# Twelve transfers of a recurrence-and-FFN kernel, issued from ScalarE's queue instead of SyncE's

## The chip, the cores and the metric

The kernel runs on one core of one Trainium2 chip. The metric is the device time of one execution in microseconds; the median of three runs before the change is 415.52 us (415.25 to 416.81). The engines are called PE (TensorE), DVE (VectorE), ACT (ScalarE), POOL (GpSimd) and SP (SyncE). Each engine works through its own list of instructions in order. SP does nothing but issue transfers (DMAs); ACT can issue transfers too, between its other instructions. Each of the two has a hardware queue of its own.

## The reference

The first half is a gated linear recurrence for 4 batches, 8 heads, 768 time steps and a head size of 48; the second half is a feed-forward network on the 3072 resulting rows of 384 features, with the maximum of three products in its middle:

```python
f = 1.0 / (1.0 + np.exp(-f_logit))
for t in range(S):
    state = f[:, :, t, :, None] * state + np.einsum('bhd,bhe->bhde', k[:, :, t], v[:, :, t])
    y[:, :, t] = np.einsum('bhd,bhde->bhe', q[:, :, t], state)
x = y.transpose(0, 2, 1, 3).reshape(B * S, H * D)
h = np.maximum(np.maximum(x @ w1, x @ w2), x @ w3)     # 384 -> 768
return h @ w_out                                       # 768 -> 384
```

The four weight matrices come as 64-bit floats; the kernel rounds them to 32 bits itself.

## The kernel before, in words

**Units and groups.** The recurrence is cut into 24 units. Unit `u` covers a chunk of 64 time steps (`c = u // 2`) of two batches (`bp = u % 2`) for all heads, so 128 tokens. Four units form a group of 512 tokens, which goes through the network together; there are six groups. While units 4 to 7 are worked on, group 0 goes through the network, and so on, one group behind.

**One unit.** `load` (L183) and `load_v` (L164) fetch f, k, q and v. From unit 6 on, f, k and q are fetched for two units at once, as eight transfers each. `sigmoids` (ACT, L311), `scan`, `after` and `before` turn them into the scaled keys `kh` and queries `qh`; DVE scans and transposes, POOL makes the products (L340 for `kh`, L351 for `qh`) and copies chunk ends (L339). `pairs` (PE, L392) multiplies `kh` by `qh`, and DVE masks the result. `values` (PE, L411) multiplies that by v, so it needs the unit's v in place. `sums` (L436) makes the next state. `finish` (PE, L500) adds what the state gives, and three ACT copies (L506) put the result into the group's tile `xT`.

**Packing.** A head has 48 features, but lies on 64 partitions. `xT` has four planes of head pairs; `pack` (L519) moves the 48 rows of the fourth plane into the gaps of the first three, by two transfers inside SBUF, so that the network's products run over three full planes of 128. It is called for units 0 to 2 of a group together and for the fourth alone, each time right after `finish`. `sums_of_x` (POOL, L854) and the network's products (PE, L870) read the packed tile.

**The network for group 0** (`ffn_first`). It runs plain products (L537) while weights are still being rounded. At its end, `place` (L454 and L461) moves the weight differences by transfers inside SBUF into a layout that fits the packed tile: ten transfers into `placed0`, ten into `placed1`, ten into a part of `w_in0`. `outputs` (PE, L563) makes the four output tiles of 128 tokens, numbered 0 to 3; ACT copies each out of PSUM (L567) and `store` (L555) sends it to the output in two transfers. Between the steps of `outputs`, POOL does `mix_in(0)` to `mix_in(3)` (L839, sums and differences of the placed weights; the first reads the first seven transfers into `placed1`), then `mix` (L587) and, during the last tile, `sums_of_x` of group 1.

**The network for groups 1 to 5.** `inputs_by_pairs` and `outputs_by_pairs` (PE, L870 and L631) save multiplications by adding and subtracting blocks beforehand, much of it on POOL. Their output stores go through `store_late`, from SP; the last group has its own, mostly from SP too.

**What sets the order.** The order is written out by hand: the loop over units calls the steps above, and between them `fill(part)` takes as many steps of the network off a list as fit a given PE time. Every engine gets its instructions in this order. Around the change, in the loop for unit 7: `finish(6)`, `pack` of units 4 to 6, `pairs(7)`, loads of f for unit 10 and of v for unit 9, `scan`, `after` and `before` of unit 8, `values(7)`; for unit 8: `finish(7)`, `pack` of unit 7, `pairs(8)`, v of unit 10, `values(8)`, k and q of unit 10. `outputs` of group 0 lie among these on PE, the `place` transfers among them on SP.

**How transfers are counted.** A transfer reports that it has landed by adding 16 to one of eight counters (named DMAHW0 to DMAHW7 in the built program). The tile framework gives the counters out in turn to all transfers of both queues, in one order that it plans when the program is built. A transfer is issued only after the previous transfer on its counter has landed: its queue waits for that count first, and for the data it needs.

## Time and profile before

| | |
|---|---|
| median of three runs | 415.52 us (415.25 to 416.81) |
| the profiled execution | 416.47 us, of which the span of its instructions is 414.6 us |
| granted PE clock, mean | 0.998 |
| busy in the span: PE, PE weight loads, DVE | 397.8, 332.4, 290.8 us |
| busy in the span: ACT, POOL | 178.7, 245.2 us |
| transfers from SP's queue | 178032 packets, 45.62 MB |
| transfers from ACT's queue | 3472 packets, 0.81 MB |

Times in the profile count from the span's first instruction. A line of a timeline gives start, length, engine, line of the program, operation, what it writes and reads, how many instructions are merged, and in brackets the idle time before it with what ended it. "SPq" and "ACTq" are transfers issued by that engine; their length is that of the issue, and the transfer lands later. A line of waits reads: who waited, for whom, microseconds in total, times, the longest.

Issues take their time on the engine that makes them: SP's mostly 0.6 to 0.65 us. From issue to landing, the profile's medians are 2.2 us for an output store, 3.2 for v, 2.6 for the large and 1.9 for the small pack, and 3.4 to 3.7 for the transfers into `placed0` and `placed1`.

### The profile page before, as it was taken

To read this page: it belongs to the slowest core of one execution; us is meant where nothing else is said; L and a number is where in the kernel's file an instruction comes from. 1 tells how busy PE (TensorE), PEld (TensorE's weight loads), DVE (VectorE), ACT (ScalarE), POOL (GpSimd) and SP (SyncE) were. 2 spreads that over 40 slices of the span, in tenths; PEclk is the share of its full clock that TensorE was granted. 3 is DMA by queue.
4 is the path that set the end of the run, shared out by engine and by line. 5 is a ranking of instruction groups with operands and counts; after the bars stand their busy time and mean duration, and the time that the engine had idled before them with its cause. 6 is when DMAs were issued, how large, how long until landed. Compare 5 with 4: busy or idle time off the path is not lost.

```text
span 414.6 us, 11546 instructions
## 1 busy us (share of the span) xinstructions
PE 397.8 (96%) x4598; PEld 332.4 (80%) x4598; DVE 290.8 (70%) x569; ACT 178.7 (43%) x412; POOL 245.2 (59%) x270
## 2 busy tenths in 40 slices
PE   4988999999999999999999999999999999999995
PEld 4766775566668889998889988889988899988984
DVE  6987897996695899898888976988894550002500
ACT  2478786511223531444541354533345324576210
POOL 2189694730989887487496376667466860435700
PEclk9999999999999999999999999999999999999999
DMA  8989987677356767377625376724473011541002
GB/s 170 237 261 273 250 231 93 86 143 159 83 104 96 122 114 132 70 118 89 137 78 104 52 117 86 163 64 80 71 146 96 2 55 44 148 136 60 0 21 62
DMA packets 181562, 47.21 MB, mean 114 GB/s; under 512 B 160448, under 2 KB 179200, under 8 KB 181504
## 3 DMA queue, kind: packets, MB, share of 16 engines
q1 hardware_dynamic: 178032, 45.62, 54.0%
q10 hardware_dynamic: 3472, 0.81, 0.9%
q8 instruction: 37, 0.61, 0.6%
q14 instruction: 21, 0.17, 0.1%
HBM read 37.75 MB, written 4.72 MB: 102 GB/s over the span
## 4 chain that ended last, share of the span: by engine, by line
PE 76%; DVE 6%; SPq 5%; POOL 3%; DMA 3%; ACT 3%; issue 2%; ACTq 0%; POOLq 0%; DVEq 0%
PE p L870 16%; PE p L631 14%; PE tr L870 13%; PE tr L631 11%; PE p L537 6%; PE p L563 3%; PE y L411 3%; PE y L500 2%; PE p L776 2%; SPq L174 2%; DMA raw<-in_moe_w_dram 2%; PE a L392 2%; PE y L436 2%; DVE ks L382 2%; SPq L164 1%
## 5 line engine op out<-in xcount | busy, mean ns | idle before, releaser
L382 DVE STREAM_TRANSPOSE ks<-kh 32x128 f32<-32x128 f32 x256 | 77.4, 302 | 11.9 <-POOL kh L340 7.7
L870 PE MATMUL tr<-xT,placed 128*128 128x256 f32 x300 | 72.6, 385 | 0.3 <-DVE hm L913 0.3
L870 PEld LDWEIGHTS tr<-xT,placed 128*128 128x128 f32 x300 | 55.7, 190 | 9.3 <-ACT hm L878 1.2
L870 PE MATMUL p<-xT,placed 128*128 128x256 f32 x180 | 45.1, 382 | 0.3 <-POOL xT L854 0.3
L339 POOL COPY ends<-r 128x8 f32<-128x8 f32 x24 | 9.8, 407 | 48.5 <-DVE r L329 48.5
L870 PEld LDWEIGHTS p<-xT,placed 128*128 128x128 f32 x180 | 33.7, 190 | 5.3 <-POOL xT L854 0.7
L537 PE MATMUL p<-xT,w_in 128*128 128x256 f32 (+1 forms) x108 | 33.9, 458 | 3.0 <-POOL w_in L745 2.2
L329 DVE TENSOR_TENSOR_SCAN r<-gate,from_one 128x520 f32<-128x520 f32 x24 | 31.5, 1314 | 6.1 <-ACT gate L308 3.0
L340 POOL TENSOR_TENSOR kh<-kt,r 128x512 f32<-128x512 f32 x18 | 30.1, 1671 | 7.6 <-DVE kt L296 6.2
L639 DVE TENSOR_TENSOR o<-tr,w_in 128x384 f32<-128x384 f32 (+1 forms) x11 | 5.7, 521 | 38.6 <-PE tr L631 35.1
L347 DVE TENSOR_TENSOR_SCAN prod<-gate,from_inv 128x520 f32<-128x520 f32 x24 | 32.1, 1336 | 0.0
L603 POOL TENSOR_TENSOR w_in<-hm 128x256 f32<-128x256 f32 x15 | 11.1, 739 | 34.9 <-DVE hm L921 32.2
L506 ACT COPY xT<-y 64x256 f32<-64x256 f32 (+1 forms) x60 | 22.1, 369 | 19.2 <-PE y L500 18.1
L870 PE MATMUL p<-w_in,placed 128*128 128x256 f32 x120 | 30.0, 379 | 0.0
L913 DVE TENSOR_TENSOR hm<-tr,hm 128x512 f32<-128x512 f32 x15 | 10.3, 688 | 26.6 <-PE tr L870 19.7
L537 PEld LDWEIGHTS p<-xT,w_in 128*128 128x128 f32 x108 | 19.5, 190 | 11.8 <-issue 6.0
L636 ACT COPY w_in<-p 128x384 f32<-128x384 f32 x15 | 7.2, 478 | 46.0 <-PE p L631 46.0
L631 PE MATMUL p<-w_in,hm 128*128 128x192 f32 x120 | 25.4, 335 | 1.1 <-ACT w_in L636 1.1
L258 POOL TENSOR_TENSOR w_in<-top_bits,rest_bits 128x384 uint32<-128x384 uint32 x18 | 21.8, 1218 | 7.6 <-DVE top_bits L252 4.7
L280 ACT ACTIVATE raw<-top_bits 128x384 f32<-128x384 f32 x48 | 25.2, 526 | 0.4
L870 PEld LDWEIGHTS p<-w_in,placed 128*128 128x128 f32 x120 | 22.8, 190 | 3.1
L631 PE MATMUL tr<-w_out,w_in 128*128 128x192 f32 x120 | 24.4, 326 | 0.0
(159 smaller groups left out, 907.6 us busy)
## 6 DMA issues: line engine op xcount, KB each, us to landing
raw<-in_moe_w_dram SPq DMA_DIRECT2D x24, 384.0 KB, 3.8
v_ld<-in_v_dram SPq DMA_DIRECT2D x48, 96.0 KB, 3.2
placed<-in_moe_w_dram SPq DMA_DIRECT2D x12, 384.0 KB, 5.4
out_dram<-o SPq DMA_DIRECT2D x46, 96.0 KB, 2.2
placed<-in_moe_w_out_dram SPq DMA_DIRECT2D x6, 384.0 KB, 6.3
f_ld<-in_f_logit_dram SPq DMA_DIRECT2D x36, 64.0 KB, 3.4
k_ld<-in_k_dram SPq DMA_DIRECT2D x36, 64.0 KB, 2.5
q_ld<-in_q_dram SPq DMA_DIRECT2D x36, 64.0 KB, 2.5
```

The costliest lines, as they stand in the source:

```text
L258: nc.gpsimd.tensor_tensor(dst, by(top), by(rest), op=ALU.add)
L280: nc.scalar.activation(over, size, AF.Relu, scale=(-1 / HI_MIN, 1.0)[step - 1], bias=(1.0, -HI_END * (1 - 2.0 ** -24))[step - 1], accum_ou ...
L329: nc.vector.tensor_tensor_scan(r[:, 0:LEN][:, ::-1], flat(gate)[:, ::-1], flat(from_one)[:, ::-1], 1.0, op0=ALU.mult, op1=ALU.max)
L340: (nc.vector if u < BY_ROWS else nc.gpsimd).tensor_tensor(kh.rearrange("p h a t -> p a h t"), kt, by_batch(r[:, 1:LEN + 1].rearrange("p (x ...
L347: nc.vector.tensor_tensor_scan(flat(prod), flat(gate_tiles[u % 2]), flat(from_inv[u % 2]), 1.0, op0=ALU.mult, op1=ALU.max)
L382: nc.vector.transpose(ks[n * 32:(n + 1) * 32, :, par, e0:e0 + 32], kh[p0:p0 + 32, :, a, t0:t0 + 32])
L411: nc.tensor.matmul(y[o:o + DP, a, hp * C:(hp + 1) * C], lhsT=v_ld[s, 2 * hp + par, :], rhs=d["at"][s, par, hp, :], start=(hp == 0), stop=F ...
L506: nc.scalar.copy(xT[o, :, t0 + a * C:t0 + (a + 1) * C], y[i, a, 0:HP * C].rearrange("p (h t) -> p h t", h=HP))
L537: nc.tensor.matmul(p if w < TOK else p.rearrange("p (two t) -> p two t", two=2), lhsT=w_in[i][:, kt, j * 128:(j + 1) * 128], rhs=x[:, t.st ...
L563: nc.tensor.matmul(p[:, 0:DM], lhsT=lhsT, rhs=rhs, start=(n == 0), stop=(n == NJ + NK - 1))
L631: nc.tensor.matmul(b[:, p * HD:(p + 1) * HD], lhsT=x, rhs=w, start=id(b) not in begun, stop=True, skip_group_check=True)
L870: nc.tensor.matmul(b[:, j * HALF:(j + 1) * HALF], lhsT=w[:, (2 * n + j) * 128:(2 * n + j + 1) * 128], rhs=x, start=begin and j == 0, stop= ...
```

## The change

Twelve transfers move from SP's queue to ACT's: the four packing transfers of group 1 (units 4 to 6 together, and unit 7), and the eight output stores of group 0. Each stands in ACT's order right behind the copies that write what it reads. The packs of groups 2 to 5, all other stores and all loads keep their queues, and no other instruction changes its place on its engine.

```diff
-            def store(u, o):
+            def store(u, o, queue=nc.sync):
                 c, bp = divmod(u, 2)
                 for a in range(2):
                     t0 = (2 * bp + a) * S + c * C
-                    nc.sync.dma_start(out=out[t0:t0 + C, :], in_=o[a * C:(a + 1) * C, :])
+                    queue.dma_start(out=out[t0:t0 + C, :], in_=o[a * C:(a + 1) * C, :])
...
                             o = o_four[:, i]
                             nc.scalar.copy(o, p[:, 0:DM])
-                            store(i, o)
+                            store(i, o, nc.scalar)
...
                     if u > GRP:
                         finish(u - 1, xT)
+                        queues = act if u <= 2 * GRP else one
                         if u % GRP == 3:
-                            pack(0, 2, xT)
+                            pack(0, 2, xT, queues)
                         elif u % GRP == 0:
-                            pack(3, 3, xT)
+                            pack(3, 3, xT, queues)
```

`act` is the pair of queues `(nc.scalar, nc.scalar)`, `one` is `(nc.sync, nc.sync)`.

## The prediction

> **What bounds the kernel now.** First the page's engine table and the waits of PE, to see what there is to win; then the timelines of SP, ACT, POOL and PE between 80 and 125 us, where the moved transfers lie.

> Page, part 1, and the longest table of PE's waits after 60 us:
> ```profile
> PE 397.8 (96%) x4598; PEld 332.4 (80%) x4598; DVE 290.8 (70%) x569; ACT 178.7 (43%) x412; POOL 245.2 (59%) x270
> PE tr L870 <- DVE hm L913: 0.3, 1, 0.3
> PE p L870 <- POOL xT L854: 0.3, 1, 0.3
> ```
> PE is full; from 60 to 200 us it waits 0.6 us in all. That is everything a smoother queue can return here, since what follows is PE-bound too.

> SP's queue (start, length, transfers):
> ```profile
> 80.34 5.13 SPq L183 DMA_DIRECT2D q_ld<-in_q_dram  x8
> 85.51 1.28 SPq L164 DMA_DIRECT2D v_ld<-in_v_dram  x2
> 86.97 1.32 SPq L454 DMA_DIRECT2D placed<-w_in  x2
> 88.33 5.04 SPq L461 DMA_DIRECT2D placed<-w_in  x8
> 93.47 1.94 SPq L164 DMA_DIRECT2D v_ld<-in_v_dram  x2
> 95.52 1.27 SPq L454 DMA_DIRECT2D placed<-w_in  x2
> 96.84 5.04 SPq L461 DMA_DIRECT2D placed<-w_in  x8
> 109.44 1.26 SPq L519 DMA_DIRECT2D xT<-xT  x2
> 117.38 2.50 SPq L555 DMA_DIRECT2D out_dram<-o  x4
> 119.97 1.35 SPq L519 DMA_DIRECT2D xT<-xT  x2
> ```
> SP issues without a break at about 0.63 us each, 10 to 18 us behind the ACT copies that it carries away:
> ```profile
> 94.59 1.14 ACT L506 COPY xT<-y 128x256 f32<-128x256 f32 x3 [1.55 <-PE y L500]
> 99.09 0.48 ACT L567 COPY o<-p 128x384 f32<-128x384 f32 x1 [3.36 <-PE p L563]
> 106.17 0.48 ACT L567 COPY o<-p 128x384 f32<-128x384 f32 x1 [6.60 <-PE p L563]
> 108.73 1.14 ACT L506 COPY xT<-y 128x256 f32<-128x256 f32 x3 [1.55 <-PE y L500]
> 349.27 0.70 ACTq L519 DMA_DIRECT2D xT<-xT  x1
> ```
> The last line is the price of an issue on ACT. POOL and PE:
> ```profile
> 104.15 1.81 POOL L839 TENSOR_TENSOR placed<-placed 128x768 f32<-128x768 f32 x1 [13.09 <-DMA w_in<-w_in]
> 107.21 1.18 POOL L351 TENSOR_TENSOR qh<-qt,prod 128x512 f32<-128x512 f32 x1
> 100.92 0.69 PE L411 MATMUL y<-at,v_ld 64*64 64x64 f32 x32
> 108.00 0.67 PE L500 MATMUL y<-qh,state 48*48 48x64 f32 x32
> 108.49 0.65 PE L392 MATMUL a<-qh,kh 48*64 48x64 f32 x32
> ```
> POOL stands 13 us at `mix_in(0)` (L839) for placed weights. Behind it in POOL's order is `qh` of unit 8 (L351), ending at 108.39; PE's `pairs(8)` (L392) takes it at 108.49. So PE has 0.1 us of slack against those placed weights.

> **The change, part by part.** *SP loses 12 issues*, about 7.6 us at 0.63. If nothing else happened the packs would land earlier (POOL's 1.9 us wait at L854 goes), q for unit 10 would come earlier (DVE waits 1.5 us for it), and PE would win back its 0.6 us.

> *ACT gains 12 issues at 0.70*, in pairs of 1.4 us. After the pack at 95.7, the stores of tiles 0 and 1 and the pack at 109.9, ACT idles 3.36, 6.60, 1.55 and 3.36 us: hidden (the 1.55 just). After tile 3 (120.8) it idles 0.85; L311, L884 and L506 slip by up to 0.6. L884 then ends at 123.2 against PE's need of its bank at 124.43: hidden. Without those idles all of it would be 8.4 us. Zero taken.

> *The counters.* This decides. In the built program of the changed kernel every transfer of both queues counts on one of eight counters, given out in turn in the planner's order, and its issue waits until the transfer eight places earlier has landed. Before, all of these were SP's own and long landed. Now ACT's twelve sit in the same row, and well ahead of where ACT really gets to them. A landed transfer adds 16, so the count that a wait asks for, divided by 16, names the transfer. Read so, SP waits for ACT:

> | SP's issue | waits for ACT's |
> |---|---|
> | 7th of 8 of q, units 8 and 9 | pack of units 4-6, first half |
> | v of unit 7, first | same pack, second half |
> | 3rd, 4th of placed0 | stores of tile 0 |
> | 9th of placed0 | store of tile 1, first |
> | v of unit 8, first | store of tile 1, second |
> | 2nd, 3rd of placed1 | pack of unit 7, both halves |
> | 5th of f, unit 10 | store of tile 2, first |
> | 1st, 3rd of k, unit 10 | stores of tile 3 |

> So SP stops after the sixth q, 80.34 + 6 x 0.64 = 84.2, for a pack that ACT can issue only when `finish(6)` is copied. Walked forward:

> 1. Copies end 95.73; packs issued at 95.76 and 96.50. Such a pack took 2.5 us from issue to landing (its second issue at 110): 98.3 and 99.0. SP stood 14 us.
> 2. SP: two q from 98.3, v of unit 7 at 99.65 and 100.3. v took 2.9 at 85: landed 103.2. PE wants it at 100.92: **stall 2.4** (with 2.6, the shortest v, and 1.9, the shortest pack: 1.5; with 3.2, the median: 2.7).
> 3. SP: placed0 from 100.95; stores of tile 0 landed (99.60 and 100.33 plus 2.2), no stop; the 8th goes at 106.5, the 9th waits for tile 1: copied at 106.17 + 2.4 + 0.48 = 109.05, stored at 109.08, landed (2.2) 111.3. Then 10th, v of unit 8 twice, placed1 first: 112.0 to 114.6.
> 4. `finish(7)`: L506 at 108.73 + 2.4, ends 112.27; packs at 112.3 and 113.03, landed (2.0 for the small one) 114.3 and 115.1. SP's 2nd and 3rd of placed1 go at 114.65 and 115.3, the 7th, the last that `mix_in(0)` reads, at 115.3 + 4 x 0.63 = 117.85.
> 5. Before, that 7th went at 99.36 (96.84 + 4 x 0.63) and POOL began 4.8 later; placed transfers landed in 2.9 to 4.4, 3.6 median. I take 3.6 + 0.4 = 4.0, the queue being less full: **L839 at 121.9 instead of 104.15, 17.7 late** (16.0 with the short landings and a stall of 1.5, 18.9 with 4.8 and 2.7).
> 6. POOL's chain to `qh(8)` follows unchanged, 4.24 us: 126.1. PE has reached `pairs(8)` at 110.9 and stands until 126.2. PE is in order, so everything after is 17.7 late; the 2.4 is inside it, since PE had that wait on the way.
> 7. Later waits: with the restart below, all on PE is 19.9 late; the stores of tiles 2 and 3 (copied at about 133 and 140.7) hold SP's f, k and q of unit 10 again; k starts at 140.7 + 2.2 = 142.9, against 124.16 + 19.9 = 144.1 for before's place in the shifted program. No new stall; the lead of POOL remains, so the 0.6 us is won.

> *The cold restart.* PE has never stood 15 us in mid-run. The nearest row is its start after 5 us of idling:
> ```profile
> 5.05 1.08 PE L291 MATMUL tr<-ident,f_ld 128*128 128x128 f32 x4 [5.05 <-DMA f_ld<-in_f_logit_dram]
> 17.92 0.60 PE L291 MATMUL tr<-ident,f_ld 128*128 128x128 f32 x4
> ```
> Groups of four took 1.06 to 1.09 until 9.9 us, 0.60 later: 4.9 us at 0.56 of the rate, 2.2 us lost. The page's clock row shows 9 throughout, so zero is the lower end; I take 2.2, the row of the same engine after idling. [...]

> Sum: 17.7 + 2.2 - 0.6 = **+19.3 us**. The profiled execution took 416.47 (span 414.6 and 1.87 around it), so one like it would take 435.8; the median of runs, 415.52, lies 0.95 lower: **434.8**.

> **The rivals.**
> - *No cold restart* (0.13): the same walk, 415.5 + 17.1 = 432.6. For it, the clock row; against, the slow transposes at the start.
> - *A second hold-up* (0.15): in step 7 the loads of unit 10 have about 1 us in hand. If stores land in 4.2 instead of 2.2, as the pair issued at 122.8 did, each such hop adds 2 us, at tile 1's store (step 3) and again at tile 3's: up to 439.
> - *Only the late v* (0.04): were `mix_in(0)` not held, 415.5 + 2.4 = 418. Against it: POOL's order puts it ahead of `qh(8)`, and it had 0.1 us of slack.
> - *Not slower* (0.06): SP is relieved and its counters do not hold it; 0.6 won, 414.9. Price and point: it needs the 7th of placed1 issued by about 99.4, so the pack of unit 7 landed by 96.9, before `finish(7)` exists (108.7). It holds only if the waits I read belong to other transfers. This is also the case that the change does what it says.

> **How the numbers follow.** The walk above has 0.62. Its own range, all short to all long: 16.0 + 0 - 0.6 to 18.9 + 2.4, so 431 to 437. With the second hold-up and a little for a longer ACT issue: 430 to 439, leaving out the last two rivals and the ends. About 0.5% (2.1 us) is what a measurement of this kernel can tell from no change: faster 0.01, same 0.05, slower 0.94.

> **What would show it.** SP without an issue from about 84 to 98 and from 107 to 111; PE waiting about 2 us at L411 for v and about 15 at L392 for POOL's qh; POOL's wait at L839 near 31 us; L631 or L870 matmuls as long as before; POOL's wait for xT at L854 gone; slow matmuls after the restart. Wrong if SP runs through 84 to 98, or if PE passes L392 without standing: then the counters were misread.

## The result and the profile after

The changed kernel takes 435.18 us (median of four runs, 434.49 to 435.93) against 415.88 us for the kernel before beside it: a ratio of 1.0462, 95% interval 1.0432 to 1.0493. It is 19.3 us slower. The prediction was 434.8 us. The profiled execution took 434.61 us with a span of 432.9 us, 18.3 us more than the span of before.

The page of the changed kernel, busy times and the granted clock of PE in forty slices of the span:

```profile
PE 400.1 (92%) x4598; PEld 333.6 (77%) x4598; DVE 290.0 (67%) x569; ACT 178.7 (41%) x412; POOL 245.0 (57%) x270
...
PEclk9999999999859999999999999999999999999999
```

The work is the same, instruction for instruction in number; PE is busy 2.3 us longer and idle for the rest of the loss. The clock row, flat before, has two low slices (8 and 5), between 108 and 130 us. PE's waits from 60 to 240 us say where the idling is:

```profile
PE a L392 <- POOL qh L351: 14.1, 1, 14.1
PE y L411 <- DMA v_ld<-in_v_dram: 2.2, 2, 1.4
PE tr L870 <- DVE hm L913: 0.3, 1, 0.3
```

One wait of 14.1 us at `pairs(8)` and one of 2.2 us for v stand where before had 0.6 us in all. The cause lies two engines away. SP's queue in the changed kernel (start, length, transfers):

```profile
80.12 18.63 SPq L183 DMA_DIRECT2D q_ld<-in_q_dram  x8
98.79 1.28 SPq L164 DMA_DIRECT2D v_ld<-in_v_dram  x2
100.25 1.32 SPq L454 DMA_DIRECT2D placed<-w_in  x2
102.25 10.04 SPq L461 DMA_DIRECT2D placed<-w_in  x8
112.39 1.40 SPq L164 DMA_DIRECT2D v_ld<-in_v_dram  x2
113.89 1.27 SPq L454 DMA_DIRECT2D placed<-w_in  x2
115.24 5.03 SPq L461 DMA_DIRECT2D placed<-w_in  x8
...
126.70 10.71 SPq L183 DMA_DIRECT2D f_ld<-in_f_logit_dram  x8
```

Eight loads of q took 5.13 us before and 18.63 now, eight transfers into `placed0` 5.04 and 10.04. A merged line's length holds the time in which SP stood between two of its issues. ACT's side of it:

```profile
94.32 1.14 ACT L506 COPY xT<-y 128x256 f32<-128x256 f32 x3 [1.55 <-PE y L500]
95.11 1.39 ACTq L519 DMA_DIRECT2D xT<-xT  x2
...
108.53 0.48 ACT L567 COPY o<-p 128x384 f32<-128x384 f32 x1 [9.22 <-PE p L563]
109.04 1.12 ACTq L555 DMA_DIRECT2D out_dram<-o  x2
```

ACT issues each transfer as soon as the copies that it reads are done. SP's seventh q goes once the first pack of 95.11 has landed (97.90 and 97.89 us in the trace, on the same counter), and its ninth `placed0` once tile 1's store of 109.04 has (111.14 and 111.12). SP's longest waits from 78 to 145 us are for ACT's transfers; before the change none of its waits there was for a transfer:

```profile
SPq L183 <- DMA xT<-xT: 13.7, 1, 13.7
SPq L183 <- DMA out_dram<-o: 8.3, 2, 6.6
SPq L461 <- DMA out_dram<-o: 5.4, 2, 4.8
```

POOL and PE take the delay on:

```profile
120.84 1.80 POOL L839 TENSOR_TENSOR placed<-placed 128x768 f32<-128x768 f32 x1 [30.05 <-DMA placed<-w_in]
```
```profile
125.09 1.13 PE L392 MATMUL a<-qh,kh 48*64 48x64 f32 x32 [14.07 <-POOL qh L351]
126.16 3.70 PE L563 MATMUL p<-w_out,hm 128*128 128x384 f32 x6
```

`mix_in(0)` on POOL starts at 120.84 instead of 104.15, `pairs(8)` on PE at 125.09 instead of 108.49, and the six products after it take 3.70 us instead of 2.20. Before the change they were:

```profile
109.06 2.20 PE L563 MATMUL p<-w_out,hm 128*128 128x384 f32 x6
```

### The profile page after: what moved, and what is told of

Its sections match the earlier page's. It is cut to its first block, busy times and chain, and to the rows that moved or that the text cites. A ratio compares the mean times of both kernels' runs of the same rounds, so it can differ in the third digit from the quotient of the medians.

```text
span 432.9 us, 11549 instructions
## 1 busy us (share of the span) xinstructions
PE 400.1 (92%) x4598; PEld 333.6 (77%) x4598; DVE 290.0 (67%) x569; ACT 178.7 (41%) x412; POOL 245.0 (57%) x270
## 4 chain that ended last, share of the span: by engine, by line
PE 76%; DVE 7%; DMA 5%; SPq 3%; issue 3%; ACT 3%; POOL 1%; ACTq 0%; DVEq 0%; POOLq 0%
PE p L870 15%; PE p L631 14%; PE tr L870 13%; PE tr L631 10%; PE p L537 6%; PE p L563 5%; PE y L411 3%; PE a L392 2%; PE y L500 2%; SPq L183 2%; PE p L776 2%; PE y L436 2%; DVE ks L382 2%; DMA xT<-xT 1%; DMA placed<-in_moe_w_dram 1%
## 5 line engine op out<-in xcount | busy, mean ns | idle before, releaser
L870 PE MATMUL tr<-xT,placed 128*128 128x256 f32 x300 | 72.7, 385 | 0.4 <-DVE hm L913 0.3
L870 PEld LDWEIGHTS tr<-xT,placed 128*128 128x128 f32 x300 | 55.6, 190 | 9.7 <-ACT hm L878 1.6
L870 PE MATMUL p<-xT,placed 128*128 128x256 f32 x180 | 45.0, 381 | 0.0
L870 PEld LDWEIGHTS p<-xT,placed 128*128 128x128 f32 x180 | 33.8, 190 | 4.7
L339 POOL COPY ends<-r 128x8 f32<-128x8 f32 x24 | 8.8, 367 | 48.7 <-DVE r L329 48.7
L347 DVE TENSOR_TENSOR_SCAN prod<-gate,from_inv 128x520 f32<-128x520 f32 x24 | 31.2, 1299 | 0.0
L870 PE MATMUL p<-w_in,placed 128*128 128x256 f32 x120 | 30.0, 379 | 0.0
L392 PE MATMUL a<-qh,kh 48*64 48x64 f32 x768 | 16.2, 223 | 14.7 <-POOL qh L351 14.1
L506 ACT COPY xT<-y 64x256 f32<-64x256 f32 (+1 forms) x60 | 22.1, 368 | 17.1 <-PE y L500 16.0
L913 DVE TENSOR_TENSOR hm<-tr,hm 128x512 f32<-128x512 f32 x15 | 10.3, 688 | 26.6 <-PE tr L870 19.7
L631 PE MATMUL p<-w_in,hm 128*128 128x192 f32 x120 | 25.4, 335 | 1.1 <-ACT w_in L636 1.1
L392 PEld LDWEIGHTS a<-qh,kh 48*64 48x64 f32 x768 | 13.8, 138 | 15.8 <-POOL qh L351 14.2
```

The lines of the kernel that those rows point to most:

```text
L347: nc.vector.tensor_tensor_scan(flat(prod), flat(gate_tiles[u % 2]), flat(from_inv[u % 2]), 1.0, op0=ALU.mult, op1=ALU.max)
L392: nc.tensor.matmul(p[t, par, hp * C:(hp + 1) * C], lhsT=kh[r, hp, a, :], rhs=qh[r, a, hp, :], start=True, stop=True)
L506: nc.scalar.copy(xT[o, :, t0 + a * C:t0 + (a + 1) * C], y[i, a, 0:HP * C].rearrange("p (h t) -> p h t", h=HP))
L631: nc.tensor.matmul(b[:, p * HD:(p + 1) * HD], lhsT=x, rhs=w, start=id(b) not in begun, stop=True, skip_group_check=True)
L870: nc.tensor.matmul(b[:, j * HALF:(j + 1) * HALF], lhsT=w[:, (2 * n + j) * 128:(2 * n + j + 1) * 128], rhs=x, start=begin and j == 0, stop= ...
```

## The experiments

The theory: the place of the transfers is harmless, but ACT's transfers share eight landing counters with SP's, and SP waits for the eighth transfer before its own. The rivals: the load that moved (bytes, packets, or ACT's issue time) costs it; or only one of the moved pieces does.

**1. The same transfers at the same places on ACT, with other counters.** Each of the twelve is given one more dependency, on an SP transfer that is issued earlier. The planner then places it later in the row in which counters are handed out. The dependency also makes ACT wait where that transfer has not landed yet: by 2.2 us for tile 1's stores (copied at 106.95, issued at 109.10), by about 0.5 us or less for the others. The numbers index SP's transfers; the recording wrapper only keeps them in a list.

```diff
+    def planned_after(ins, n):
+        if n is not None:
+            tc.add_manual_dep(ins.ins, issued[n].ins.name, mybir.DependencyInfo(
+                mybir.DependencyClass.Sync, mybir.DependencyReason.DATA), reason="counter order")
...
-                    queues[par].dma_start(out=xT[p0 + D:p0 + DP, 0:NK, t], in_=xT[p0:p0 + D, NK, t])
+                    ins = queues[par].dma_start(out=xT[p0 + D:p0 + DP, 0:NK, t], in_=xT[p0:p0 + D, NK, t])
+                    if queues is act:
+                        planned_after(ins, [112, 131][u0 == 3])
...
-                    queue.dma_start(out=out[t0:t0 + C, :], in_=o[a * C:(a + 1) * C, :])
+                    ins = queue.dma_start(out=out[t0:t0 + C, :], in_=o[a * C:(a + 1) * C, :])
+                    if queue is nc.scalar:
+                        planned_after(ins, [116, 127, 136, 144][u])
```

> The twelve transfers stay on ACT's queue, at the same places in ACT's order. Each gets one added dependency on an earlier transfer of SP, chosen so that it has about landed when ACT arrives; this puts ACT's transfers later in the order in which the eight counters are given out, so that SP's transfers wait only for ones of ACT that have about landed. Counter theory: SP runs through 84 to 98 us, POOL's mix_in(0) starts within 0.5 us of 104.15, PE does not stand at pairs(8), and the time is that of the kernel before, 415.3 to 416.5 (0.3 won at L854, up to 0.5 lost on holds of SP). Rival, that ACT's queue, ACT's issue time or the early transfers themselves cost the time: it stays 10 us or more above before.

Measured: 415.54 us against 416.41 before, ratio 0.997 (0.9953 to 0.9987). The whole loss is gone, with all twelve transfers still on ACT. Lines of code sit 14 to 18 lower in this kernel, and SP's issues all have the line of the wrapper, L94. Its SP queue, POOL and PE:

```profile
80.91 4.96 SPq L94 DMA_DIRECT2D q_ld<-in_q_dram  x8
...
95.54 9.96 SPq L94 DMA_DIRECT2D placed<-w_in  x10
```
```profile
105.86 1.81 POOL L857 TENSOR_TENSOR placed<-placed 128x768 f32<-128x768 f32 x1 [14.51 <-DMA placed<-w_in]
```
```profile
PE a L406 <- POOL qh L365: 1.2, 1, 1.2
```

q flows again (4.96 us). The ten transfers into `placed1` still take 9.96 us instead of the 6.31 (1.27 + 5.04) of before, because the fifth of them now meets, in the built program, the counter of the first pack of units 4 to 6, which ACT issued at 96.18 us. So `mix_in(0)` starts 1.7 us later than before (0.3 of it was late from the program's start on), not within 0.5 as expected, and PE waits 1.2 us: the same mechanism, small.

A second, longer comparison of the same kernel:

> The same kernel as the run ordered, to see whether its 0.3% below the kernel before stands: counter theory with the relief of SP: 0.3 to 0.6 us below before at the waits of PE on POOL's L854 and DVE, ratio 0.996 to 0.999. If the first was chance: 1.000 inside the interval.

Measured: 415.03 us against 416.04, ratio 0.9982 (0.9964 to 1.0). Both point to 0.2 to 0.3% faster, which is within the 0.5% that a measurement of this kernel can tell from no change.

Where that small gain comes from: from the copy of tile 3 to the copies (L506) of `finish(12)`, the profile of before takes 63.87 us (120.32 to 184.19) and this one 61.96 (122.02 to 183.98), so 1.9 us came back although PE's list of waits had only 0.6 to give. (It was 1.7 us late at tile 3, so the span gained only 0.3.) PE's weight loads have a list of their own. In the kernel before, from 120 to 185 us:

```profile
PEld p L870 <- POOL xT L854: 0.7, 1, 0.7
...
PEld tr L870 <- DVE hm L913: 0.5, 1, 0.5
```

Neither line is in the list of the reordered kernel. All lines of that list add up to 4.6 us before and to 2.8 us (122 to 184 us) in the reordered kernel: 1.8 less, close to the 1.9. In the changed kernel they make 4.3 us (139 to 203 us), with the second of the two lines still there, and the same way takes 63.57 us: 0.3 less of both. The two go together, but no run changes one alone, so that the weight loads are the cause of the gain is not shown.

**2. Transfers of 4 bytes on ACT, everything else as before.** The kernel before, with all its transfers left on SP; ACT issues twelve transfers of one element at the places of the change, into a tile that nobody reads.

```diff
+            crumbs = keep.tile([128, 16], FP32, name="crumbs")
+            n_crumbs = [0]
+
+            def tiny(src, wanted=True):
+                for _ in range(2 if wanted else 0):
+                    n = n_crumbs[0]
+                    nc.scalar.dma_start(out=crumbs[0:1, n:n + 1], in_=src)
+                    n_crumbs[0] = n + 1
...
                             store(i, o)
+                            tiny(o[0:1, 0:1])
...
                             pack(0, 2, xT)
+                            tiny(xT[0:1, NK, 2 * UT:2 * UT + 1], u <= 2 * GRP)
                         elif u % GRP == 0:
                             pack(3, 3, xT)
+                            tiny(xT[0:1, NK, 3 * UT:3 * UT + 1], u <= 2 * GRP)
```

> The kernel before, with all twelve transfers on SP as before, and twelve new transfers of 4 bytes each issued by ACT at the places where the change puts its own; nobody reads what they write. Counter theory: they take the same places in the row of counters, SP stands from about 84 to 98 us again, and the time is near the changed kernel's, +16 to +20 us. Rival, that it is the moved data's way through ACT's queue or where it lands: within 1 us of before. ACT's issue time alone: under 1 us by its idle times.

Measured: 442.1 us against 416.41, ratio 1.0612 (1.0588 to 1.0636): 25.7 us slower, for 48 bytes. Its SP queue and PE's waits:

```profile
80.84 17.63 SPq L183 DMA_DIRECT2D q_ld<-in_q_dram  x8
...
126.97 10.17 SPq L183 DMA_DIRECT2D f_ld<-in_f_logit_dram  x8
```
```profile
PE a L392 <- POOL qh L351: 13.9, 1, 13.9
PE p L880 <- POOL xT L864: 6.7, 1, 6.7
```

Bytes are out as a cause: the first hold is there in full. What exceeds the expectation is a second hold, the 6.7 us of the second line, with slow products once more behind it: four at 149.69 us took 2.07 us, where four at 139.03 us had taken 1.03. Here the pack of unit 7 is still on SP, issued at 145.33 us, behind the held f, held loads of v and four stores, and what it packs is needed for group 1 (L864 is `sums_of_x`, L880 its products). In the changed kernel that pack has left SP, so the same stop of f (10.71 us) costs PE next to nothing.

**3. One part of the change at a time.** Four kernels, each the changed one with a part returned to SP; their diffs in the order of the table:

```diff
-                        queues = act if u <= 2 * GRP else one
+                        queues = act if u < 2 * GRP else one
...
-                            store(i, o, nc.scalar)
+                            store(i, o)
```
```diff
-                        queues = act if u <= 2 * GRP else one
+                        queues = act if u == 2 * GRP else one
...
-                            store(i, o, nc.scalar)
+                            store(i, o)
```
```diff
-                            store(i, o, nc.scalar)
+                            store(i, o)
```
```diff
-                        queues = act if u <= 2 * GRP else one
+                        queues = one
```

Pack of units 4 to 6 alone:

> Only the two packs of units 4 to 6 go to ACT. Counter theory: v of unit 7 and the 1st of placed0 wait for them (to 98.3 and 99), then SP runs on without a stop; the 7th of placed1 goes at 111.0, mix_in(0) starts at 114.1, 9.9 late, and with 2.0 for the clock the kernel is 11.6 us slower.

Pack of unit 7 alone:

> Only the two 24 KB packs of unit 7 go to ACT; the packs of units 4 to 6 and all stores stay on SP. Counter theory: the 2nd and 3rd transfer into placed1 wait for them, so SP stands from 96 to about 113, mix_in(0) starts about 3 us after the 7th of placed1 goes at 115.5: 118.6, 14.4 late, and with 2.0 for the slow clock after it the kernel is some 16 us slower; v of unit 7 is on time. If the cost goes with the number or bytes of moved transfers (2 of 12): about 3 us.

Both packs:

> Only the four packs of group 1 go to ACT; the stores stay on SP. Counter theory: v of unit 7 and the 1st of placed0 wait for the first pack (to 98.3 and 99), the 2nd and 3rd of placed1 for the second (to 113.2 and 114); the 7th of placed1 goes at 116.5, mix_in(0) starts at 119.6, 15.4 late, PE waits 1.0 for v of unit 7, and the kernel is 17.1 us slower. If the parts added up, this and the stores alone would make 19 together.

The eight stores alone:

> Only the eight output stores of group 0 go to ACT; the packs stay on SP. Counter theory: the 3rd and 4th of placed0 wait for tile 0's stores (to about 102.5), v of unit 8 and the 1st of placed1 for tile 1's (to about 109.6); the 7th of placed1 goes at 114, mix_in(0) starts at 117.1, 12.9 late, and with 2.0 for the clock the kernel is 14.6 us slower.

| on ACT | time, us | ratio (interval) | `mix_in(0)` starts | PE's waits |
|---|---|---|---|---|
| pack of units 4 to 6 | 428.66 | 1.0309 (1.0274 to 1.0344) | 116.34 | L411 1.8, L392 7.7 |
| pack of unit 7 | 430.57 | 1.0335 (1.0311 to 1.0359) | 117.45 | L392 13.2 |
| both packs | 431.11 | 1.0368 (1.0332 to 1.0404) | 118.30 | L411 1.3, L392 13.0 |
| the stores | 437.5 | 1.0522 (1.0474 to 1.057) | 118.01 | L392 13.4, L870 5.0 |
| all twelve | 435.18 | 1.0462 (1.0432 to 1.0493) | 120.84 | L411 2.2, L392 14.1 |

The first three cost 13.1, 14.2 and 15.6 us, where 11.6, about 16 and 17.1 were expected. Two transfers alone cost 13 to 14 us, and the parts add up to far more than the whole (13.1 + 14.2 + 22.0 against 19.3). SP was held until the latest of the transfers that it met, so the parts overlap: with both packs `mix_in(0)` starts at 118.30 us, with one of them at 116.34 or 117.45. With the pack of unit 7 alone, SP runs freely up to `placed1` and stops there, in one line:

```profile
93.23 18.81 SPq L454 DMA_DIRECT2D placed<-w_in  x2
```

The stores alone are worse than the whole change, which was not expected (some 15 us were, 22.0 came). Their first hold is as expected; then, at 124 us, comes the second:

```profile
124.69 11.37 SPq L183 DMA_DIRECT2D f_ld<-in_f_logit_dram  x8
136.10 4.28 SPq L164 DMA_DIRECT2D v_ld<-in_v_dram  x2
140.48 1.30 SPq L519 DMA_DIRECT2D xT<-xT  x2
```
```profile
PE p L870 <- POOL xT L854: 5.0, 1, 5.0
```

It is that of experiment 2: the pack of unit 7, left on SP, waits behind transfers that wait for the stores of tiles 2 and 3. Moving the packs as well, harmful alone, spares the kernel this one.

**4. What the wait costs beyond its length.** The changed kernel with products of no use ahead of `pairs(8)`, so that PE does not idle there: `busy(n)` issues n products that the kernel uses at its start too.

```diff
+                    if u == 2 * GRP:
+                        busy(56)
                     pairs(u)
```

> The changed kernel with 56 idle matmuls of 256 columns put on PE ahead of pairs(8), 12 us of work in its 14 us wait; nobody reads their result. If the slow matmuls after the wait come from PE's clock after idling: granted clock 1.00 from 126 us on, the first six L563 in 2.1 instead of 3.7 us, and 2.0 us faster than the changed kernel, +17 against before. If they come from something else (transfers, POOL and DVE working beside): no change, +19.

Measured: 445.22 us, ratio 1.0684 (1.0648 to 1.0719). One such product is two instructions of about 0.22 us, so 56 of them take 24.44 us and overrun the wait by some 10. As a measure of the total it says nothing; but from `pairs(8)` to the copy of tile 2 this kernel needs 4.80 us (134.61 to 139.41), the kernel before 4.75 (108.49 to 113.24), the changed one 6.74 (125.09 to 131.83). With 26 products, beside the changed kernel again:

> As the run with 56 idle matmuls, which took 24.4 us instead of the 12 meant and overran the wait by 10, but with 26 of them, 11.3 us by what the 56 took, inside the 14 us wait. Clock theory: pairs(8) starts when POOL's qh ends as in the changed kernel, the granted clock stays at 1.00, the way from pairs(8) to the copy of tile 2 takes 4.8 us instead of 6.7, and the kernel is 2.0 us faster than the changed one: +17.0 to +17.5 against before. Something else beside the clock: +19.

> The changed kernel beside the others on one chip, for the 2.0 us of warm26: ratio to before 1.046, 18.5 to 19.3 us above it.

Measured: 435.98 us (1.0475, 1.0451 to 1.0499) and 437.24 us (1.0498, 1.0466 to 1.0529). That is 19.9 and 21.2 us above before, where 17.0 to 17.5 and 18.5 to 19.3 were expected. The 26 products end 3.2 us too early, and the clock falls all the same: it read 1.00 from 128 to 129 us, 0.54 from 129 to 130 and 0.50 from 130 to 132, so it fell at about 129.08 us, 1.3 us after PE took up work again. From `pairs(8)` to the copy of tile 2 it is 6.49 us. So this pair does not settle it. The third pair does, with 31 products:

> The changed kernel with 31 idle matmuls (62 instructions of 0.221 us in the run with 26, so 13.7 us) ahead of pairs(8), against a wait of 14.1 to 14.7 us: TensorE should idle at most about 1 us there. If the cold restart is what the wait costs beyond its length, the granted clock stays at 1.00 from 120 to 135, the six products at L563 behind it take 2.2 us instead of 3.6 to 3.8, and the span is about 2.0 us below that of the changed kernel beside it. If an idle of that size or some other cause slows the products, they take 3.5 us or more again and the time is the same within 0.5 us. The short wait for v at L411 (2.2 us) stays and may or may not drop the clock by itself (0 or 1.7 us).

> The changed kernel as it is, beside the one with the idle matmuls: about 435 to 437 us, 18 to 21 us over the kernel before; wait at L392 of 14.1 to 14.6 us, then products at L563 in 3.6 to 3.8 us. Whether the clock drops after the wait of 2.2 us at L411 too decides between the low and the high end.

Measured: 435.86 us (432.6 to 436.76; ratio 1.0469, 1.0432 to 1.0507) and, for the changed kernel beside it, 438.64 us (436.57 to 440.06; 1.0529, 1.0478 to 1.058), 22.2 us above before where 18 to 21 were expected. PE with the 31 products, and then the changed kernel beside it:

```profile
110.62 13.65 PE L968 MATMUL p<-from_one,ident 128*128 128x256 f32 x62
125.21 0.69 PE L392 MATMUL a<-qh,kh 48*64 48x64 f32 x32 [0.95 <-POOL qh L351]
125.84 2.20 PE L563 MATMUL p<-w_out,hm 128*128 128x384 f32 x6
```
```profile
104.93 3.75 PE L563 MATMUL p<-w_out,hm 128*128 128x384 f32 x6
...
127.46 1.13 PE L392 MATMUL a<-qh,kh 48*64 48x64 f32 x32 [14.17 <-POOL qh L351]
128.52 4.21 PE L563 MATMUL p<-w_out,hm 128*128 128x384 f32 x6
```

With PE kept busy the products take 2.20 us, the clock is 1.00 throughout, and it is 4.80 us from `pairs(8)` to the copy of tile 2, as before the change; the changed kernel beside it needs 7.31 (127.46 to 134.77). So the cold clock cost 2.0 to 2.5 us after the long wait. The medians differ by 2.8 us with intervals that overlap; the lines of the profile carry this, not the medians.

The line at 104.93 shows something else. It follows the wait for v (2.6 us in this profile) and is slow as well, 3.75 us against 2.20. In the first profile of the changed kernel the same products after the same wait (2.2 us) took 2.20. Stretches of 4 us in that first profile and in this one (the columns behind the length: PE, PEld, DVE, ACT and POOL busy, granted clock, DMA share, GB/s):

```profile
104.00:108.00 4.00, 4.00 (x39) 2.50 (x31) 0.56 (x1) 0.00 (x0) 0.00 (x0) 1.00 0.62 159
```
```profile
104.00:108.00 4.00, 4.00 (x66) 2.61 (x65) 0.56 (x1) 0.00 (x0) 0.00 (x0) 0.68 0.46 116
```

The granted clock was 1.00 in the one and 0.68 in the other. Tile 1's copy then comes 1.7 us later (6.93 us behind the second part of `values(7)` instead of 5.24), and with it tile 1's store and SP's ninth `placed0`. Of three profiles of the changed kernel two have this second cold stretch. It goes some way to explain why its medians lie at 435.18, 437.24 and 438.64 us in three comparisons.

## Why the prediction was right

**The counters.** Right, and they are the cause. In the trace SP stands until ACT's transfers on its counters have landed; experiment 1 takes the loss away with all twelve still on ACT and other counters (one pair of stores also goes 2.2 us later there), and experiment 2 makes the loss with 48 bytes and nothing moved.

| step of the prediction | predicted | profile after |
|---|---|---|
| 1: SP stopped till | 98.3 | v of unit 7 issued at 98.79, after two q |
| 2: wait at L411 | 2.4 (1.5 to 2.7) | 2.2 |
| 3: v of unit 8, behind the ninth and tenth `placed0` | about 112 | 112.39 |
| 4: seventh `placed1` | 117.85 | 117.8 (115.24 + 4 x 0.63) |
| 5: `mix_in(0)` | 121.9, 17.7 late | 120.84, 16.7 late |
| 6: `pairs(8)` | 126.2 | 125.09, 16.6 late |
| cold restart | 2.2 | 2.0 (6.74 - 4.75) |
| 7: won back later | 0.6 | 0.3 |
| sum, in the span | +19.3 | +18.3 |

**Mis-sized terms.** Step 5 took 4.0 us from the issue of the seventh `placed1` to the start of POOL (3.6 for landing and 0.4); it was 3.1 (117.8 to 120.84), 2.7 of it landing; why that was shorter than before, no run shows. This is the largest error, 0.9 of the 1.0 in the sum. The restart's 2.2 us, from PE's start, was a good measure: 2.0, 2.1 and 2.5 in the three profiles of the changed kernel. The zero that the flat clock row allowed was wrong: here the row fell. At the program's start the row could not show it, since the trace of before holds no record of the clock ahead of 10.18 us, just where the slow products end.

Step 3 has two slips without a price, as SP waits for tile 1's store in any case. Seven issues of 0.63 us after 100.95 bring the eighth `placed0` to 105.4, not 106.5 (it went at 105.84). And the stores of tile 0 took 2.9 and 3.0 us to land, not 2.2, so that SP did stand for them, 0.6 us.

**Step 7** was right that no new stall comes. DVE waits 2.3 and 2.8 us for the loads of unit 10 (149 and 154 us), where it waited 3.5 and 1.5 before the change (131 and 136 us): about as much in all. PE's later waits did not grow, and the time from tile 3's copy to `finish(9)`'s copies fell from 17.54 to 17.25 us, half of the 0.6 predicted. The statement that a smoother queue could return 0.6 us at most was too low: experiment 1 got 1.9 us back, while the waits of the weight loads, which the prediction had not read, fell by 1.8.

**What the sum left out.** The wait for v was taken as plain waiting inside the later one. In two profiles of three it also cooled the clock, worth 1.6 and 1.7 us on the path. That the median of 435.18 lies within 0.4 us of the forecast is partly two errors that cancel: the profiled sum was 1.0 us lower than predicted, and the median lies 0.6 above the profiled execution, where the forecast had put it 0.95 below.

**The rivals.** No cold restart: refuted by the clock (0.50 at 124 to 129 us) and by experiment 4. Only the late v: refuted by the 14.1 us at L392. A second hold-up: it exists at SP (f took 10.71 us), without a price in this kernel, and with PE waits of 5.0 and 6.7 us where the pack of unit 7 stayed on SP. Not slower: its condition, SP not held, is what experiment 1 makes, and the time then is 415.0 to 415.5 us, near the 414.9 named for it.

## What to carry to other kernels

Before a transfer is moved to another queue, list in the built program which transfers of the old queue will share its landing counter, and compare when each of the two can really be issued: here a transfer that came late held the eighth one after it in the planned row, whoever issued that, SP for 13.7 us at the longest. The size of the transfer did not matter for this (4 bytes were enough), and the parts of such a move, priced one by one, did not add up. If the move itself is wanted, fix its place in the planned row (here by one more dependency each), and look at the weight loads' waits too for what there may be to win.

## What the runs showed of the hardware

The granted clock in stretches of the three profiles of the changed kernel (from and to, in us):

| profile | granted clock |
|---|---|
| first | 104 to 110: 1.00; 110 to 126: 0.67; 126 to 129: 0.50; 129 to 130: 0.89; 130 to 132: 1.00 |
| second | 104 to 110: 0.72; 110 to 126: 0.65; 126 to 132: 0.50; 132 to 134: 1.00 |
| third | 104 to 108: 0.68; 108 to 112: 0.89; 112 to 116: 0.96; 116 to 132: 0.50; 132 to 136: 0.91 |

Shorter waits did the same in some executions. Behind the wait for v at L411 the clock read less than 1.00 (0.50 to 0.86 in stretches of 2 us) between 104 and 108 us in four profiles, and the six products there took 3.42 to 3.83 us; in five others it read 1.00 from 102 to 108 us, and they took 2.20:

| wait at L411, us | profile | six products behind it, us |
|---|---|---|
| 1.1 | 4 bytes on ACT | 2.20 |
| 1.3 | both packs | 2.20 |
| 1.3 | 56 products | 2.20 |
| 1.5 | 31 products | 2.20 |
| 1.8 | pack of units 4 to 6 alone | 3.42 |
| 2.2 | changed kernel, first | 2.20 |
| 2.3 | changed kernel, second | 3.83 |
| 2.5 | 26 products | 3.82 |
| 2.6 | changed kernel, third | 3.75 |

With 26 products the clock fell after the 3.2 us at L392 as well. Each of these five falls cost 1.6 to 1.7 us. The length of the wait alone does not sort them: 1.8 us was followed by a fall and 2.2 us was not. Why, no run shows.
